# A recurrence, a mixture of experts and a feed-forward layer on one core: router steps, scatters and DMAs in another order

## The chip, the cores and the metric

The kernel runs on one core of a Trainium2 chip. The metric is the time of one execution in device microseconds (us); lower is better. In the text PE is TensorE, DVE is VectorE, ACT is ScalarE, POOL is GpSimd and SP is SyncE. SP computes nothing here: it issues most of the DMAs and reads register values.

## The reference

Three layers follow one another. Everything is float32.

```
# 1. recurrence over 768 steps, for 4 batches x 8 heads, head_dim 48
cur        = outer(u * k[t], v[t])
y[t]       = r[t] @ (state + cur)
state      = w[t][:, None] * state + outer(k[t], v[t])
# 2. x = y as 3072 tokens x 384; 8 experts, one per token
e          = argmax(x @ w_gate);  gate = softmax(x @ w_gate)[e]
x2[token]  = gate * sigmoid((x @ w_output_gate)[e]) * (relu(x @ w1[e]) @ w2[e])      # w1: 384x1024
# 3. dense layer, 384 -> 2048 -> 384
out        = relu(x2 @ w_in) ** 2 @ w_out
```

## The kernel before

**Stage 1, the recurrence (0 to about 180 us).** It is done in chunks of 128 steps. A unit is one pair of heads of one batch, so there are 16 units, and units 4b to 4b+3 are batch b. The loop over t runs from -1 to 16 and is a software pipeline: in one turn PE does the score products of unit t, the output of unit t-1, and the transposes of unit t+1. The order of the work on all five engines is the order of the calls in the text (a manual schedule), so an engine that waits holds everything behind it on that engine. The calls of one turn that matter here: `scores` (PE products into PSUM, ACT copies them to `A`, POOL masks them by an affine select, L734 to L737), `states` and `state_scan` (PE L744, DVE L749 into `St`), `suffix` and `prefix` (four DVE scans, L687 and L693), `k_turn` and `r_turn` (PE transposes L667, then DVE products `kT` L702 and `rA` L707), `gate_sum` and `gate_values` (DVE sum L717 of products that POOL made at L712 and L713, then POOL L720), `within` and `across` (PE L765 and L775, then ACT copies `xT` L777). The PSUM buffers of the transposes and the scores are one ring of four.

**The router.** When a batch is done, a generator (`route_steps`) computes its experts and ranks in 13 steps; two tables, `PLAN` for batches 0 and 1 and `LAST` for batch 2, say at which (turn, place) a step is taken; the places of a turn are "back", "scan", "turned", "gate" and "end". Steps 3 and 4 stand at (5, "scan") and hold small DVE operations and two ACT exponentials, `ez` (L188) and `sg` (L202). The last six steps each issue one scatter (POOL, L245) of 128 token rows into `x_rows` in DRAM, each row with 384 values, the gate factor and the token number. Batch 3 is routed after the loop.

**Stage 2, the experts (about 180 to 400 us).** Up to 320 tokens of expert 0 from batches 0 to 2 are block A; they are gathered (POOL, L400) after batch 2's scatters and worked on while batch 3 is routed. After batch 3's six scatters the experts are sorted by count. Block 0 is a rest of up to 128 tokens of expert 0, in rows (`up_rows`, `turn`, `down_rows`); blocks 1 to 7 are the other experts. A block's rows are gathered from `x_rows`, scaled (block 1's on DVE, L411), transposed on PE (`prep_x`, L430), and go through eight steps f of `up` (PE, 9 products of 128x128 weights, L344 to L346), a relu (ACT L333, DVE L334) and `down`. Each matrix is split into a high and a low float32r part (ACT cast L337, DVE or POOL difference L339). A block's words come in two halves of 1.5 MB (`load(0)`, `load(1)`: `w1r` L324 and `w2r` L325, two DMAs of 768 KB on SP); the first half serves f = 0 to 3.

**The order of DMAs on SP around the end of routing.** SP issues block 1's `load(0)`, then all engines pass a branch over rare cases (L941 to L942); at its end SP waits until all its own DMAs have landed. Then SP reads nine register values (L559, L562), stores block 0's token numbers (`put_ids`: 128 numbers of 4 bytes to `x2_ids`, L480), issues block 1's `load(1)`, the first load of a conversion (`convert_load`, `cq`, L1075), block A's results in three parts (`put_A`, L1238), with block 1's token numbers (384 and 96 of them, L480 and L484) ahead of the second part. The row gathers of blocks 0 and 1 are issued by POOL.

**Stage 3, the dense layer (about 400 to 846 us).** It goes over the 3072 tokens in 6 groups of 512, twice over halves of the 2048 columns, with PE in use throughout.

Of the kernel before, what the change touches and what calls it, by code (L numbers as in the profile page):

```python
# [9 lines left out]
F32 = mybir.dt.float32  # L10
# [11 lines left out]
def rwkv_moe_kernel(  # L22
# [15 lines left out]
    nc = tc.nc  # L38
# [522 lines left out]
    def expert_of(k):  # L561
        return nc.values_load(bei[0:1, k:k + 1], engines=(ET.SP,), min_val=0, max_val=E - 1)  # L562
# [13 lines left out]
    with ExitStack() as actx:  # L576
# [208 lines left out]
        def at(i, st, *a):  # L785
            if 0 <= i < NU:
                getattr(units[i], st)(*a)
# [1 line left out]
        PLAN = ((4, "gate"), (5, "back"), (5, "scan"), (5, "scan"), (6, "back"), (6, "scan"), (7, "scan"),  # L789
                (7, "turned"), (7, "gate"), (8, "back"), (8, "turned"), (9, "back"), (9, "turned"))  # L790
        LAST = ((4, "gate"), (5, "back"), (5, "scan"), (5, "scan"), (5, "turned"), (5, "gate"), (6, "scan"),
                (6, "scan"), (6, "turned"), (6, "gate"), (6, "end"), (7, "back"), (7, "scan"))

        def step(t, place):
            for b in range(B - 1):
# [42 lines left out]
        for t in range(-1, NU + 1):  # L838
            z = first_z if t == -1 else zw
            load("w", w, t + 3)  # L840
            if t >= 0:
                load("v", v, t + 1)
                load("k", k, t + 2)
                load("r", r, t + 2)
            first_block_step(t, "loads")
            at(t, "scores", 0)
            at(t, "k_back")
            at(t + 2, "w_check")
            step(t, "back")
            first_block_step(t, "back")  # L850
            if t + 1 < NU - 1:
                at(t + 1, "gate_products")
            at(t + 1, "suffix", 1, z)
            at(t + 1, "prefix", 1, z)
            at(t - 1, "within")
            at(t, "states")
            at(t, "state_scan")
            step(t, "scan")
            at(t, "scores", 1)
            at(t + 1, "spread")  # L860
            at(t - 1, "across")
            at(t + 1, "k_turn")
            at(t + 1, "r_turn")
            step(t, "turned")
            first_block_step(t, "turned")
            at(t + 2, "w_turn")
            at(t, "bonus_in")
            if t + 1 == NU - 1:
                at(t + 1, "gate_products")
            at(t + 1, "gate_sum")  # L870
            at(t + 1, "gate_values")
            at(t + 2, "suffix", 0)
            at(t + 2, "prefix", 0)
            step(t, "gate")
            first_block_step(t, "gate")
            if t < NU:
                at(t - 1, "back")
            step(t, "end")
# [27 lines left out]
    with tc.manual_schedule(engines={ET.PE, ET.DVE, ET.Activation, ET.SP, ET.Pool}):  # L906
        put_ids_A()
        blkA.prep_w(FA, nc.vector)
        route_step()
        route_step()  # L910
        blkA.up(0)
        route_step()
        route_step()
        route_step()
        blkA.up(1)
        nc.vector.tensor_scalar(flag[:, 0:1], pf[:1, :1], 0.0, None, op0=ALU.is_le)
        blkA.down(0)
        more = None
        while more is None:
            nc.gpsimd.memset(warm, 0.0)  # L920
            more = route_step()
        tc.mark_branch_hint_location("rare", "LikelyTaken", [ET.PE, ET.DVE, ET.SP])
        finish = finish_routing()
        next(finish)
        blkA.prep_w1(FA + 1, nc.vector)
        blkA.prep_w2(FA + 1, part="hi")
        for f in range(2, FA):
            blkA.up(f)
            if f == 2:
                next(finish)  # L930
                next(finish)
                blk1 = block_of(P, 1, expert_of(1))
                blk1.load(0)
            blkA.down(f - 1)
        for _ in finish:
            pass
        blkA.down(FA - 1)
# [261 lines left out]
    with tc.manual_schedule(engines={ET.PE, ET.DVE, ET.Activation, ET.SP, ET.Pool}):  # L1199
        block_rows()  # L1200
        blocks = [block_of(P, 0, 0), blk1]
        blk0 = blocks[0]
# [4 lines left out]
        for f in range(FA, KF):  # L1207
            blkA.up(f)
            if f + 2 < KF:
                blkA.prep_w(f + 2, nc.vector)  # L1210
            if f > FA:
                blkA.down(f - 1)
            if f == FA:
                blkA.prep_w2(FA + 1, nc.vector, part="lo")
            if f == FA + 1:
                for k in range(1, E):
                    if k == 1:
                        blk1.words_of(expert_of(k))
                    else:
                        blocks.append(block_of(P, k, expert_of(k)))  # L1220
                    blocks[k].banks((k + 1) % 2)
                blk0.put_ids(lambda: column(off, 0))
                blocks[1].load(1)
                convert_load(0)
            if f == KF - 1:
                blk0.prep_x(0)
# [18 lines left out]
        blk0.turn(0)  # L1245
        for f in range(2):
            blocks[1].prep_w1(f)
        blocks[1].put_ids(lambda: column(off, 1))
        put_A(1)
        convert_load(1)  # L1250
        put_A(2)
        blocks[1].prep_x(0)
        blk0.down_rows(0)
# [7 lines left out]
        for n in range(KF, E * KF):  # L1261
# [12 lines left out]
                nxt.gather(range(2 * f, min(2 * f + 2, nxt.nt)))  # L1274
            if e == 1 and f == 2:
                blk0.put(column(off, 0))
            if f == 2 and prev:
                prev.put(column(off, e - 1))
                if e == E - 1:
                    load_x(0)  # L1280
# [105 lines left out]
```

## Time and profile before

| what | value |
|---|---|
| median of 3 runs | 845.77 us (844.73 to 846.93) |
| the profiled execution's own time | 848.16 us |
| its span (first to last instruction) | 846.3 us |
| PE busy, share of the span | 808.7 us, 96% |
| PE weight loads | 733.0 us, 87% |
| DVE / ACT / POOL busy | 533.8 / 374.6 / 351.9 us |
| mean granted TensorE clock | 0.984 |
| HBM traffic, mean | 120 GB/s |

The profile page divides the span into 40 slices; PE is busy for nine tenths or more in nearly all of them, and less so in the first slice and in two slices around 180 and 210 us. The clock of TensorE has two levels, 1.2 and 2.4 GHz; the profile gives it as a share, 0.50 or 1.00 (or a mean of the two over a stretch). Busy time of PE is modelled at its ends, so the waits that the timeline notes beside an instruction, as [us <-who ended it], say more than the busy share.

### The profile page before, as it was taken

What the parts mean: (1) busy time and instruction counts of PE and PEld (TensorE: products, weight loads), DVE (VectorE), ACT (ScalarE), POOL (GpSimd) and SP (SyncE); (2) the same over time, 40 slices, a digit from 0 to 9 for tenths busy, and PEclk for the clock granted to TensorE, in tenths of its full rate; (3) what the DMA queues carried; (4) which work ended last, traced back from release to release, by engine and by line L of the source; (5) the groups of instructions that cost most, each with busy time, mean ns of one, the idle gap of its engine ahead of it and who ended that gap; (6) DMA issues with size and microseconds to landing.
All of it is one profiled execution on the core that took longest, in us unless ns stands there. A gap on an engine that the chain in (4) does not pass through costs nothing.

```text
span 846.3 us, 15487 instructions
## 1 busy us (share of the span) xinstructions
PE 808.7 (96%) x5868; PEld 733.0 (87%) x5868; DVE 533.8 (63%) x961; ACT 374.6 (44%) x792; POOL 351.9 (42%) x433
## 2 busy tenths in 40 slices
PE   6999999988799999999999999999999999999995
PEld 5988888868688999999999998888899999999994
DVE  7889888875367678787733788888633434434342
ACT  4666565632344554555554434343433333333321
POOL 8566767534245355555554234333311212223121
PEclk9999999999899999999999999999999999999998
DMA  8675759315967477577762232323204123032010
GB/s 179 131 151 108 168 116 222 134 53 161 151 189 213 129 246 209 151 227 237 151 195 63 94 112 65 105 79 108 75 1 140 35 79 112 9 104 76 1 47 37
DMA packets 157362, 102.89 MB, mean 122 GB/s; under 512 B 112348, under 2 KB 140940, under 8 KB 157284
## 3 DMA queue, kind: packets, MB, share of 16 engines
q1 hardware_dynamic: 149044, 86.55, 38.9%
q0 software_dynamic: 4912, 14.65, 5.0%
q8 instruction: 47, 0.77, 0.4%
q10 hardware_dynamic: 3328, 0.66, 0.4%
q14 instruction: 31, 0.25, 0.1%
HBM read 79.34 MB, written 22.50 MB: 120 GB/s over the span
## 4 chain that ended last, share of the span: by engine, by line
PE 69%; issue 13%; DVE 8%; POOL 4%; DMA 4%; ACT 1%; POOLq 0%; DVEq 0%; SPq 0%; ACTq 0%
PE ph L345 9%; PE ph L344 9%; PE ph L346 9%; PE po L344 5%; PE px L344 5%; PE px L346 5%; PE po L346 5%; PE po L345 5%; PE px L345 5%; POOL out_dram L1177 2%; PE py L765 2%; PE pt L667 2%; PE pt L734 2%; DMA xg<-x_rows,gi 2%; DMA x_rows<-xr,dsi 2%
## 5 line engine op out<-in xcount | busy, mean ns | idle before, releaser
L1152 DVE SCALAR_TENSOR_TENSOR gg<-ph,rl 128x512 f32<-128x512 f32 x96 | 66.2, 689 | 121.7 <-ACT rl L1150 121.7
L1150 ACT ACTIVATE rl<-ph 128x512 f32<-128x512 f32 x96 | 57.5, 599 | 146.5 <-PE ph L346 146.3
L339 DVE TENSOR_TENSOR gl<-gg,gh 128x512 fp32r<-128x512 f32 x96 | 66.8, 696 | 65.9 <-ACT gh L337 41.9
L337 ACT CAST gh<-gg 128x512 fp32r<-128x512 f32 x96 | 59.6, 621 | 103.5 <-DVE gg L1152 103.5
L339 POOL TENSOR_TENSOR w1l<-w1r,w1h 128x384 fp32r<-128x384 f32 x56 | 59.4, 1067 | 70.2 <-ACT w1h L337 69.7
L333 ACT ACTIVATE hh<-ph 128x320 fp32r<-128x320 f32 (+7 forms) x64 | 32.5, 508 | 112.9 <-PE ph L346 104.1
L1098 POOL TENSOR_TENSOR caf<-caf,cbf 128x384 f32<-128x384 f32 x32 | 32.6, 1018 | 114.0 <-DVE cbf L1097 114.0
L339 DVE TENSOR_TENSOR w2l<-w2r,w2h 128x384 fp32r<-128x384 f32 x64 | 64.9, 1016 | 20.0 <-ACT w2h L337 19.5
L334 DVE SCALAR_TENSOR_TENSOR hl<-ph,hh 128x320 fp32r<-128x320 f32 (+7 forms) x64 | 36.8, 576 | 36.9 <-ACT hh L333 36.6
L1177 POOL DMA_INDIRECT out_dram<-ob,tokc x24 | 23.4, 974 | 67.2 <-DVE ob L1175 65.0
L344 PE MATMUL po<-hh,w2h 128*128 128x320 f32 (+4 forms) x120 | 42.3, 353 | 0.0
L345 PE MATMUL po<-hl,w2h 128*128 128x320 f32 (+4 forms) x120 | 41.3, 345 | 0.0
L346 PE MATMUL po<-hh,w2l 128*128 128x320 f32 (+4 forms) x120 | 41.2, 344 | 0.0
L339 POOL TENSOR_TENSOR x22l<-x2r,x22h 128x512 fp32r<-128x512 f32 x12 | 15.5, 1293 | 51.5 <-ACT x22h L337 51.5
L737 POOL TENSOR_SCALAR_AFFINE_SELECT A<-A 128x768 f32<-128x768 f32 x32 | 27.9, 872 | 18.9 <-ACT A L736 18.8
L400 POOL DMA_INDIRECT xg<-x_rows,gi x28 | 28.9, 1033 | 15.6 <-DMA x_rows<-xr,dsi 9.3
L339 POOL TENSOR_TENSOR x21l<-x2r,x21h 128x512 fp32r<-128x512 f32 x12 | 15.5, 1294 | 45.5 <-ACT x21h L337 45.5
L734 PE MATMUL pt<-rA,kT 64*128 64x128 f32 x300 | 32.2, 307 | 2.1 <-DVE rA L707 2.1
L337 ACT CAST w2h<-w2r 128x384 fp32r<-128x384 f32 x64 | 33.0, 516 | 0.0
L245 POOL DMA_INDIRECT x_rows<-xr,dsi x24 | 24.4, 1019 | 20.2 <-DVE vals L238 14.1
L337 ACT CAST w1h<-w1r 128x384 fp32r<-128x384 f32 x64 | 32.7, 512 | 0.0
L339 POOL TENSOR_TENSOR x20l<-x2r,x20h 128x512 fp32r<-128x512 f32 x12 | 15.5, 1292 | 35.9 <-ACT x20h L337 35.9
(859 smaller groups left out, 2665.1 us busy)
## 6 DMA issues: line engine op xcount, KB each, us to landing
w1r<-in_moe_w_dram SPq DMA_DIRECT2D x16, 768.0 KB, 7.2
w2r<-in_moe_w_dram SPq DMA_DIRECT2D x16, 768.0 KB, 8.6
x2r<-x_cols SPq DMA_DIRECT2D x12, 768.0 KB, 4.9
cq<-in_moe_w_in_dram SPq DMA_DIRECT2D x16, 384.0 KB, 4.3
cq<-in_moe_w_out_dram SPq DMA_DIRECT2D x16, 384.0 KB, 5.9
vN<-in_v_dram SPq DMA_DIRECT2D x32, 144.0 KB, 3.9
part<-ob SPq DMA_DIRECT2D x24, 192.0 KB, 1.9
ob<-part SPq DMA_DIRECT2D x24, 192.0 KB, 2.5
```

Source lines behind the costliest of these rows:

```text
L333: nc.scalar.activation(hi, src, AF.Relu)
L334: nc.vector.scalar_tensor_tensor(lo, src, 0.0, hi.bitcast(F32), op0=ALU.max, op1=ALU.subtract)
L337: nc.scalar.copy(hi, src)
L339: lo_eng.tensor_tensor(lo, src, hi.bitcast(F32), op=ALU.subtract)
L344: nc.tensor.matmul(out_, a_of(ah), b_of(bh), start=start, stop=False)
L345: nc.tensor.matmul(out_, a_of(ah), b_of(bl), start=False, stop=False)
L346: nc.tensor.matmul(out_, a_of(al), b_of(bh), start=False, stop=stop)
L734: nc.tensor.matmul(pa[j][:, ci], self.kT[pp, hf * HC + ci], self.rA[pp, hf * HC + ci], start=True, stop=True)
L1098: nc.gpsimd.tensor_tensor(af, af, bf, op=ALU.add)
L1150: nc.scalar.activation(rl, ph, AF.Relu)
L1152: nc.vector.scalar_tensor_tensor(gg, ph, 0.0, rl, op0=ALU.max, op1=ALU.mult)
L1177: ins = nc.gpsimd.indirect_dma_start(out=out[:, :], out_offset=IndirectOffsetOnAxis(ap=tokc[:, n:n + 1], axis=0), in_=ob, in_offset=None)
```

## The change

Six things are done in another place; nothing is computed otherwise.

1. In a turn of the loop, the router steps of the place "scan" come after `scores(t, 1)`, `spread(t+1)` and `across(t-1)`, no longer before them.
2. Unit 0's `gate_sum` and `gate_values` come in turn 0 after unit 1's four scans, no longer in turn -1 ahead of them.
3. In `LAST` the last scatters of batch 2 come earlier: two at (6, "turned"), two at (6, "gate"), one at (7, "scan"), none at (6, "end") or (7, "back").
4. Ahead of block 1's `load(0)` SP issues a DMA of 4 bytes from `x_rows` into `spare`, a tile that nothing else of this path uses. As a reader of `x_rows` it waits for scatters of batch 3, and `load(0)` is queued behind it.
5. Block 0's and block 1's `put_ids` move from there to block 1's steps f = 2 and f = 3.
6. `convert_load(1)` comes ahead of the second part of block A's results.

```diff
         LAST = ((4, "gate"), (5, "back"), (5, "scan"), (5, "scan"), (5, "turned"), (5, "gate"), (6, "scan"),
-                (6, "scan"), (6, "turned"), (6, "gate"), (6, "end"), (7, "back"), (7, "scan"))
+                (6, "scan"), (6, "turned"), (6, "turned"), (6, "gate"), (6, "gate"), (7, "scan"))
...
             at(t + 1, "suffix", 1, z)
             at(t + 1, "prefix", 1, z)
+            if t == 0:
+                at(t, "gate_sum")
+                at(t, "gate_values")
             at(t - 1, "within")
             at(t, "states")
             at(t, "state_scan")
-            step(t, "scan")
             at(t, "scores", 1)
             at(t + 1, "spread")
             at(t - 1, "across")
+            step(t, "scan")
...
-            at(t + 1, "gate_sum")
-            at(t + 1, "gate_values")
+            if t >= 0:
+                at(t + 1, "gate_sum")
+                at(t + 1, "gate_values")
...
                 blk1 = block_of(P, 1, expert_of(1))
+                nc.sync.dma_start(spare[:, 0:1].bitcast(F32), x_rows[0:1, 0:1])
                 blk1.load(0)
...
-                blk0.put_ids(lambda: column(off, 0))
                 blocks[1].load(1)
                 convert_load(0)
...
-        blocks[1].put_ids(lambda: column(off, 1))
+        convert_load(1)
         put_A(1)
-        convert_load(1)
+        at1 = [column(off, 1)]
         put_A(2)
...
             if e == 1 and f == 2:
                 blk0.put(column(off, 0))
+                blk0.put_ids(lambda: column(off, 0))
+            if e == 1 and f == 3:
+                cur.put_ids(lambda: at1.pop() if at1 else column(off, 1))
```

DVE at the start of the loop, end of turn -1 and turn 0 (`g` is the gate sum, `suf` and `ff` are the scans of unit 1, `St` is unit 0's state scan):

```order
 L707 TENSOR_TENSOR rA<-pa,ff 128x6x64
+L687 SCALAR_TENSOR_TENSOR suf<-zw,s_142 128x388
+L692 RECIPROCAL f_141<-suf 128x3
+L693 SCALAR_TENSOR_TENSOR ff<-zw,f_141 128x387
+L687 SCALAR_TENSOR_TENSOR suf<-zw,s_142 128x388
+L692 RECIPROCAL f_141<-suf 128x3
+L693 SCALAR_TENSOR_TENSOR ff<-zw,f_141 128x387
 L717 TENSOR_REDUCE g<-g_256 128x12
```

The gate sum stood ahead of these six and now stands behind them, just ahead of the state scan.

ACT in the turn of batch 0's router steps 3 and 4, turn 5 (batches 1 and 2 alike, turns 9 and 13):

```order
 L178 COPY lg<-pt 128x2x3x16
+L736 COPY A_1213<-pt 128x3x128
+L736 COPY A_1213<-pa 128x3x128
+L697 COPY P_147<-suf 128x48x5
+L777 COPY xT<-py 128x384 x2
 L188 ACTIVATE ez<-z 128x48
 L202 ACTIVATE sg<-zs 128x6
-L736 COPY A_1234<-pt 128x3x128
-L736 COPY A_1234<-pa 128x3x128
-L697 COPY P_147<-suf 128x48x5
-L777 COPY xT<-py 128x384 x2
```

The two exponentials wait for DVE's router operations; they stood ahead of the copies of the scores and now stand behind them and behind the `xT` copies. On DVE the order of this turn is the same as before.

SP before, at the end of the register values after the rare branch:

```order
L559 TENSOR_LOAD off
L559 ISA x2
L480 REGISTER_ALU
L480 DMA x_ids<-xg_4903 128x1x1
L324 ISA
L324 DMA w1r<-in_moe_w_dram 128x3x512
L325 ISA
L325 DMA w2r<-in_moe_w_dram 128x4x384
L1075 DMA cq<-in_moe_w_in_dram 128x3x256
L1238 DMA x_cols<-yT 128x3x128
```

SP with the change, ahead of the rare branch (`spare`) and then in block 1's steps f = 2 and 3, after block 0's results (`yT_5294`):

```order
L946 TENSOR_LOAD flag
L946 ISA x2
L937 DMA spare<-x_rows 1x1
L324 ISA
L324 DMA w1r<-in_moe_w_dram 128x3x512
L325 ISA
L325 DMA w2r<-in_moe_w_dram 128x4x384
L947 COMPARE_AND_BRANCH
```

```order
L489 DMA x_cols<-yT_5294 128x3x128
L559 TENSOR_LOAD off
L559 ISA x2
L480 REGISTER_ALU
L480 DMA x_ids<-xg_4904 128x1x1
L480 REGISTER_ALU
L480 DMA x_ids<-xid 128x3x1
L559 TENSOR_LOAD off
L559 ISA x2
L484 ISA
L484 DMA x_ids<-xid 96x1
```

The small read stands ahead of the first half of block 1's words, and the three stores of token numbers are gone from the place between the register values and the second half.

## Rows read from the trace of the kernel before

**Rows 1.** Windows: PE, PEld, DVE, ACT, POOL busy us; PEclk, DMA share, GB/s.

```profile
200.00:250.00 50.00, 42.97 (x222) 38.10 (x220) 23.04 (x43) 20.57 (x49) 17.81 (x18) 0.92 0.72 154
```

**Rows 2.** Timeline of PE: start, us, line, operation [idle before <-releaser].

```profile
209.30 0.33 PE L430 MATMUL px<-ident,xg 128*128 128x128 f32 x1 [1.05 <-DMA xg<-x_rows,gi]
221.99 0.43 PE L430 MATMUL po<-ident,xg 96*128 96x96 f32 x1 [5.87 <-DVE xg L411]
222.12 0.67 PE L344 MATMUL px<-w2h,hh 128*128 128x384 f32 x1
225.79 0.60 PE L503 MATMUL px<-ident,hh 128*128 128x128 f32 x4
227.12 0.44 PE L344 MATMUL px<-w2h,hh 128*128 128x384 f32 x1
229.69 0.38 PE L344 MATMUL ph<-x0h,w1h 128*128 128x480 f32 x1
```

**Rows 3.** Windows of 2 us in that stretch.

```profile
216.00:218.00 2.00, 0.12 (x2) 0.00 (x0) 0.00 (x0) 1.29 (x3) 1.04 (x2) 1.00 0.88 52
222.00:224.00 2.00, 2.00 (x7) 1.89 (x8) 1.32 (x4) 0.56 (x1) 0.00 (x0) 0.50 1.07 389
```

**Rows 4.** Chain that ended last, 192 to 222 us: start us, us, what.

```profile
211.29 10.20 DMA xg<-x_rows,gi
```

**Rows 5.** Timeline of SP, its DMA issues, 188 to 262 us.

```profile
194.62 0.40 SPq L325 DMA_DIRECT2D w2r<-in_moe_w_dram  x1
210.77 0.57 SPq L480 DMA_DIRECT2D x_ids<-xg  x1
```

**Rows 6.** Timeline of POOL, last scatter and first gather after it.

```profile
195.97 0.97 POOL L245 DMA_INDIRECT x_rows<-xr,dsi  x1 [0.22 <-issue]
206.21 0.98 POOL L400 DMA_INDIRECT xg<-x_rows,gi  x1 [9.27 <-DMA x_rows<-xr,dsi]
```

**Rows 7.** Landing: tile x_rows (150 to 262 us), tile w2r (185 to 262).

```profile
DMA to landing us min/median/max: 2.6/3.9/10.2
DMA to landing us min/median/max: 9.3/9.3/9.4
```

**Rows 8.** DMA queues, 196 to 200 us: packets, MB, share.

```profile
q1 hardware_dynamic: 752, 1.32, 86.9%
q0 software_dynamic: 66, 0.21, 12.8%
```

**Rows 9.** SP, end of the rare branch: count, ns, first and last start.

```profile
L942 SPq EVENT_SEMAPHORE  x9: 17/17/17, 196.9 to 204.2; - x9
```

**Rows 10.** Timeline of ACT, block 1: words 4, rows of block 2.

```profile
234.58 0.51 ACT L337 CAST w1h<-w1r 128x384 fp32r<-128x384 f32 x1
246.33 2.13 ACT L413 ACTIVATE xg<-xg 128x384 f32<-128x384 f32 x4
```

**Rows 11.** Timeline of PE in the three units with router steps.

```profile
67.08 0.27 PE L667 MATMUL pt<-ident,rN 64*128 64x64 f32 x1 [0.93 <-ACT A L736]
107.42 0.97 PE L667 MATMUL pt<-ident,rN 64*128 64x64 f32 x12 [1.95 <-ACT A L736]
149.47 0.97 PE L667 MATMUL pt<-ident,rN 64*128 64x64 f32 x12 [1.94 <-ACT A L736]
```

**Rows 12.** Timeline of DVE after the third of them.

```profile
150.41 1.02 DVE L707 TENSOR_TENSOR rA<-pt,ff 128x384 f32<-128x384 f32 x2 [0.51 <-PE pt L667]
158.09 0.76 DVE L749 TENSOR_TENSOR_SCAN St<-pt,P 128x288 f32<-128x288 f32 x1 [0.60 <-PE pt L744]
```

**Rows 13.** Timeline of DVE, then of PE, at the start of the kernel.

```profile
13.13 0.75 DVE L717 TENSOR_REDUCE g<-g 128x12 f32<-128x576 f32 x1 [2.03 <-POOL g L713]
18.74 0.37 PE L667 MATMUL pt<-ident,kN 64*128 64x64 f32 x1 [1.25 <-DVE St L749]
```

**Rows 14.** Timeline of PE, then of POOL, in the last unit.

```profile
173.24 0.88 PE L765 MATMUL py<-A,vN 128*64 128x128 f32 x12 [2.37 <-POOL bia L920]
174.81 0.99 POOL L400 DMA_INDIRECT xg<-x_rows,gA  x1 [1.61 <-DVE w2l L339]
```

## The prediction

> **What bounds the kernel now.** I read the page first (PE is busy almost throughout), then the windows by stage, which show where it is not: between 200 and 250 us PE is busy for 42.97 of 50 us at a mean granted clock of 0.92 [rows 1], and after 250 us no slice has a gap. Then the timeline of PE, for each wait and what ended it. The reader is to see that four small groups of waits in the first 230 us are all that an order can win; after them PE runs without a pause to the end, so a microsecond won before 230 us is a microsecond of the whole.
>
> The largest wait is at 216.1 to 222.0 us: PE waits 5.87 us for the last of block 1's gathered rows [rows 2]. The chain says why: that gather left POOL at 211.29 and took 10.20 us [rows 4], against 2.6 us for the quickest DMA on that table [rows 7]. It was issued 0.52 us after SP had stored block 0's token numbers (210.77, [rows 5]). In the middle of that time the DMA engines are busy for 0.88 of their time and move only 52 GB/s, where they move 389 GB/s six microseconds later [rows 3]. What fills them with next to nothing is, I read, the store of 128 numbers of 4 bytes. After this wait the granted clock stands at 0.50 (1.2 GHz) [rows 3], and the 12 products that follow take 3.67 us (222.12 to 225.79) where the next 12 of the same kind take 2.57 us (227.12 to 229.69) [rows 2].
>
> Ahead of that, POOL issues the last scatter at 195.97 and waits until 206.21 for them to land [rows 6], while SP's first half of block 1's words, issued up to 194.62 [rows 5], flows beside them.
>
> **The change part by part.**
>
> *Unit 0's gate sum.* DVE waits 2.03 us for POOL's products ahead of four scans; PE waits 1.25 us for the state scan behind them [rows 13]. With the sum behind the scans, POOL's products are ready before DVE comes to them, so the 2.03 us go. Late next is PE itself, which stood still for only 1.25 us. I take 1.2 us; the ends are 0 (another input is late) and 2.0.
>
> *Router steps 3 and 4 later on ACT.* In three turns PE waits for ACT's copies of the scores, 0.93, 1.95 and 1.94 us [rows 11], since ACT sits before `ez` and `sg`, which wait for DVE. Behind the copies they hold nobody: their results are read by router steps that come at least a place later. DVE's order is unchanged, so DVE caps the gain where it is nearly full: after the third turn its idle time is 0.51 + 0.60 = 1.11 us [rows 12]. Hence 0.9 + 1.9 + 1.1 = 3.9 us. The ends: 1.5 us (0.51 us per turn, if DVE decides everywhere) and 4.8 us (the three waits in full).
>
> *Batch 2's scatters.* PE waits 2.37 us for POOL's last mask, which stands behind scatters; block A's gather leaves at 174.81 [rows 14]. With the scatters earlier the mask comes some 2 us earlier, but block A's first transposes and, behind them, batch 3's logits still need the gathered rows, and one scatter stays between mask and gather. PE's wait moves to those rows. I take 0; the ends are 2.4 us and a loss of 1.0 us, about the clock's price after the other wait (3.67 - 2.57 us).
>
> *The small read ahead of block 1's words.* It adds one DMA of 4 bytes and a wait on SP for scatters. The last one leaves POOL's queue at 195.97 + 0.97 and should land 2.6 to 3.9 us after its start [rows 6, 7], so near 199.5 where POOL saw them landed at about 206. The words then leave near 200.3 and 201 where they left at 194.62, and POOL's gathers of blocks 0 and 1 leave between about 200.5 and 206. So the words no longer run beside the scatters, but beside the gathers. Between 196 and 200 us the words' queue moved 752 packets and the scatters' 66 [rows 8]: the gathers will creep until the words are in, 9.4 us after their issue [rows 7], near 210.4. Block 0's rows may come as late as before, where PE waits 1.05 us [rows 2]: I take 0, between a gain of 1.05 and a loss of 2 us (landing 1 us after the words). The Trainium skill, "DMA: Bandwidth & Descriptors", section "Queues, rings and completion order", says that each DMA engine takes turns between the queues that have work, packet by packet. By that rule the gathers would get their turn beside the words and the 1.05 us would go; the trace's 66 against 752 packets speak against equal turns.
>
> Behind the waiting SP stand the words, the rare branch and all that follows it. At the end of that branch SP waits for its own DMAs, before until 204.2 [rows 9], now until about 210.4. From there it needed 6.6 us of register reads and one wait to reach its next DMA (210.77); so the second half of the words leaves near 217 and lands by 226.4. ACT casts the first of them at 234.58 [rows 10], 7.0 us earlier by the sum below, 227.6. That is free by 1.2 us; if it lands 3 us later than that, it costs about 2 us.
>
> *Token numbers later.* The two blocks' stores leave the time of the gathers, and nothing else clogs the engines there: the last of block 1's rows can be in by about 214, before PE wants it at 216.1. So the 5.87 us go, and with them the 1.1 us at the low clock: 7.0 us. The ends are 0 (the gathers creep until PE waits as long) and 7.0. The three stores are not saved: they follow in block 1's steps 2 and 3, behind block 0's results and block 2's first words on the same queue, where no wait of PE shows now. The moved conversion load is needed 20 us later and costs nothing.
>
> *Sum.* 1.2 + 3.9 + 0 + 0 + 7.0 = 12.1 us. The profiled execution's own time is 848.16 us, 2.4 above the median of the runs; against it this is 836.1, and against the median of 845.77 it is **833.7 us**.
>
> **The rivals.**
>
> 1. *Equal turns on the DMA engines.* The gathers share evenly with the words, as the rule above has it, and block 0's wait goes too: 833.7 - 1.05 = 832.6 us. Against it stands the share of packets [rows 8].
>
> 2. *The wait only moves.* The gathers creep behind the words and SP's late second half adds to it, so PE waits as long for rows or words as it did for the last gather; only the recurrence gains: 845.8 - 1.2 - 3.9 = 840.7 us. For it: the scatters that ran beside the words landed late [rows 6]. Against it: 5 us lie between the words' landing and PE's need.
>
> 3. *DVE takes over in the recurrence.* The waits of PE for ACT become waits for DVE and only the expert stage gains: 845.8 - 7.0 = 838.8 us. For it: 1.11 us of idle time after the third turn. Against it: PE's waits at the other two are longer than DVE's work behind them asks.
>
> 4. *The stores hold up block 2's rows, and the kernel gets slower.* Block 2's rows are gathered in block 1's steps 0 and 1 and scaled on ACT at 246.33 [rows 10], or 239.3 when shifted. The stores would come near 229.5. If a store holds a gather as the one at 210.77 held the last one until 221.5, for 10.7 us, and the three of them do so in turn, the rows land at 229.5 + 32.1 = 261.6: a wait of 22.3 us and 1.1 for the clock, less 12.1, is 857 us. It decides from rows later than about 253 on; two stores in turn (250.9) would make the time that of before. Against it: block 2's last gather leaves about when the first store does, ahead of most of their writes.
>
> 5. *It doesn't do what it says.* The read waits for only some of the scatters, or the late landing had another cause, and no wait goes: 845.8 us.
>
> **How the numbers follow.** Forecast 0.64, rival 1 0.08, rival 2 0.14, rival 3 0.06, rival 4 0.04, rival 5 0.04. About 0.3% (2.5 us) is what a measurement of this kernel tells from no change. The first four cases are faster: 0.92; rival 5 is the same, 0.04; rival 4 slower, 0.04. All upper ends together (2.0 + 4.8 + 2.4 + 1.05 + 7.0 = 17.2) would give 828.6, which asks for everything at once; I take 829. Upwards the range reaches to rival 2, 841. It leaves out rivals 4 and 5 and the tails of the rest, under 2 in 10.
>
> **What would show each step.** In the changed profile: DVE's gate sum of unit 0 behind the scans with no wait of 2 us; ACT's copies of the scores ahead of `ez` in turns 5, 9 and 13 and no wait of PE of 0.9 to 2 us there; the wait of PE for POOL's mask in the last unit gone, and one for block A's rows in its place; the words of block 1 issued after the scatters have landed, POOL's first gather of block 0 some 6 us nearer to the last scatter; block 1's last rows landing without a stretch of full DMA engines at 50 GB/s, and no wait of 5.87 us nor a clock of 0.50 behind it; that stretch in block 1 instead, without a wait of PE. The prediction is wrong if block 0's or block 1's rows still arrive after PE asks for them by more than 2 us, if ACT waits for the second half of the words, or if the turns of the recurrence are as long as before.

## The result, and the profile after

The changed kernel takes 837.37 us (median of 4 runs, 836.17 to 837.66), the kernel before on the same chip 846.35 us (844.73 to 848.15): a ratio of 0.9891, 95% interval 0.9867 to 0.9914, 9.0 us faster. The forecast was 833.7 us with a range of 829 to 841. The profiled execution of the changed kernel has a span of 835.6 us, 10.7 less than before. Single times of one kernel spread by 0.6 to 6.4 us, those of the kernel before by more (841.7 to 853.8 over all its runs). So a verdict is taken from medians, and a microsecond is read from traces, each of which shows one execution only.

The windows of the changed kernel (columns as in [rows 1]), the stage of [rows 1] first, then the end of the recurrence:

```profile
200.00:250.00 50.00, 49.47 (x259) 42.89 (x258) 29.90 (x53) 24.05 (x56) 20.17 (x21) 1.00 0.64 177
...
170.00:174.00 4.00, 0.49 (x4) 0.14 (x1) 1.10 (x3) 0.37 (x1) 2.66 (x3) 1.00 0.39 105
174.00:178.00 4.00, 2.85 (x14) 1.60 (x16) 2.42 (x9) 1.18 (x3) 0.00 (x0) 0.50 0.11 19
178.00:182.00 4.00, 4.00 (x23) 3.25 (x19) 1.93 (x9) 1.47 (x5) 0.00 (x0) 0.50 0.01 0
182.00:186.00 4.00, 4.00 (x18) 3.82 (x18) 2.54 (x14) 0.45 (x2) 0.00 (x0) 0.50 0.00 0
186.00:190.00 4.00, 4.00 (x24) 4.00 (x24) 2.62 (x13) 1.67 (x4) 3.19 (x6) 0.80 0.28 99
```

Between 200 and 250 us PE is now busy for 49.47 us at full clock (42.97 at 0.92 before, [rows 1]). But there is a new hole: from 170 to 174 us PE works for 0.49 of 4 us, and behind it the granted clock stands at 0.50 (1.2 GHz) until about 187.6 us.

The timeline of PE in the changed kernel: the first `within`, the last `across` but one, the last router products, block A's rows, the branch, block 0's rows, block 1's last rows, block 1's first product.

```profile
22.46 1.53 PE L765 MATMUL py<-A,vN 128*64 128x128 f32 x24
...
162.49 1.41 PE L775 MATMUL py<-rA,St 64*64 64x128 f32 x20
...
168.26 1.93 PE L169 MATMUL pt<-xT,wcat 128*32 128x256 f32 x24
173.53 0.30 PE L430 MATMUL pt<-ident,xg 128*128 128x128 f32 x1 [3.34 <-DVE xg L411]
174.74 0.47 PE L430 MATMUL pt<-ident,xg 128*128 128x128 f32 x1 [0.91 <-DVE xg L411]
175.50 1.28 PE L430 MATMUL pt<-ident,xg 64*128 64x64 f32 x4 [0.28 <-DVE xg L411]
...
195.95 0.38 PE L344 MATMUL ph<-x0h,w1h 128*128 128x320 f32 x1 [1.29 <-PEq L947]
205.31 0.27 PE L430 MATMUL px<-ident,xg 128*128 128x128 f32 x1
211.57 0.57 PE L430 MATMUL po<-ident,xg 128*128 128x128 f32 x4
212.46 0.44 PE L344 MATMUL px<-w2h,hh 128*128 128x384 f32 x1 [0.31 <-ACT hh L337]
...
218.96 0.38 PE L344 MATMUL ph<-x0h,w1h 128*128 128x480 f32 x1
```

In the kernel before the same points lie like this on PE (up to the branch; block 0's rows and block 1's first product are in [rows 2]):

```profile
24.67 1.53 PE L765 MATMUL py<-A,vN 128*64 128x128 f32 x24
...
167.01 1.40 PE L775 MATMUL py<-rA,St 64*64 64x128 f32 x20
...
176.38 2.50 PE L169 MATMUL pt<-xT,wcat 128*32 128x256 f32 x24
...
179.84 0.33 PE L430 MATMUL pt<-ident,xg 128*128 128x128 f32 x1 [0.70 <-DVE xg L411]
180.63 0.84 PE L430 MATMUL pt<-ident,xg 64*128 64x64 f32 x4 [0.46 <-DVE xg L411]
...
197.20 0.38 PE L344 MATMUL ph<-x0h,w1h 128*128 128x320 f32 x1 [1.97 <-PEq L942]
```

So PE is 2.2 us early at 22 us, 4.5 us early at the last `across` but one, 8.1 us early at the router's last products, only 1.25 us early at the branch, and 10.7 us early at block 1's first product (229.69 in [rows 2]). From there to the end both traces take 616.6 us. Neither the 1.05 us wait for block 0's rows nor the 5.87 us wait for block 1's is left [rows 2]. For block A's rows PE now waits 3.34 + 0.91 + 0.28 = 4.5 us, where it waited 0.70 + 0.46 = 1.2 us before.

What PE waits for between 20 and 165 us in the changed kernel (us in total, times, longest): the three waits of [rows 11] for ACT's scores, 4.8 us in all, are gone. Waits for DVE have come in their place, 5.1 us in the list below, where the kernel before has 1.0 us of them in the same window. The longest, 1.95 us at 144.30 us, stands in the turn of the third wait of [rows 11].

```profile
PE pt L209 <- DVE kT L702: 1.9, 1, 1.9
PE pt L734 <- DVE rA L707: 1.7, 5, 0.3
PE pt L667 <- DVE kT L702: 1.0, 3, 0.6
PE pt L209 <- ACT A L736: 0.5, 2, 0.3
PE pa L667 <- DVE kT L702: 0.5, 1, 0.5
```

The timelines of POOL (block A's first gather, the last scatter, block 0's first gather) and of SP (the read, block 1's first words, its second half, the token numbers) in the changed kernel, for [rows 5, 6, 14]:

```profile
169.77 1.00 POOL L400 DMA_INDIRECT xg<-x_rows,gA  x1 [3.73 <-issue]
192.84 0.97 POOL L245 DMA_INDIRECT x_rows<-xr,dsi  x1 [0.22 <-issue]
198.82 1.07 POOL L400 DMA_INDIRECT xg<-x_rows,gi  x1 [5.00 <-DVE hl L334]
```

```profile
195.49 0.30 SPq L937 DMA_DIRECT2D spare<-x_rows  x1
196.06 0.44 SPq L324 DMA_DIRECT2D w1r<-in_moe_w_dram  x1
...
210.71 0.39 SPq L324 DMA_DIRECT2D w1r<-in_moe_w_dram  x1
...
226.28 0.58 SPq L480 DMA_DIRECT2D x_ids<-xg  x1
237.38 0.41 SPq L480 DMA_DIRECT2D x_ids<-xid  x1
```

The gather follows the last scatter by 5.98 us (198.82 - 192.84), where it was 10.24 us [rows 6]. Block A's gather is only 5.0 us earlier than in [rows 14], although PE comes to it 8.1 us earlier: POOL stands 3.73 us between the last scatter (164.88) and the gather, and the gathered rows are what DVE, and behind it PE, wait for. I take the 3.73 us for the landing of that scatter, but the trace has no landing time for it, and those just ahead of it landed in 2.6 to 2.7 us; so it is not shown that the landing is all of it.

### The profile page after: what moved, and what is told of

Read it like the earlier page. It is cut to its first block, busy times and chain, and to the rows that moved or that the text cites. A ratio compares the mean times of both kernels' runs of the same rounds, so it can differ in the third digit from the quotient of the medians.

```text
span 835.6 us, 15492 instructions
## 1 busy us (share of the span) xinstructions
PE 805.9 (96%) x5868; PEld 731.1 (87%) x5868; DVE 534.2 (64%) x961; ACT 374.3 (45%) x792; POOL 352.3 (42%) x433
## 4 chain that ended last, share of the span: by engine, by line
PE 59%; issue 12%; POOL 4%; DVE 0%; POOLq 0%; ACT 0%; DVEq 0%; ACTq 0%
PE ph L345 10%; PE ph L344 10%; PE ph L346 10%; PE po L344 5%; PE po L346 5%; PE po L345 5%; PE px L346 5%; PE px L344 5%; PE px L345 5%; POOL out_dram L1182 2%; PE px L430 1%; PE po L430 0%; POOL x22l L339 0%; POOL x21l L339 0%; POOL x20l L339 0%
```

## The experiments

The theory at this point: two chains of work race to block 0's rows. One is PE's own. The other goes through block A's rows, batch 3's logits, its scatters and block 0's gathers. What the recurrence won is partly lost in the hole at 170 us and at the low clock behind it, and it is lost on the second chain too, since batch 3's logits stand behind block A's rows on PE. Rivals are the prediction's own sum, each term worth what it said, and that the hole costs nothing. All experiments ran beside the kernel before; the ratio is that of the times to it. They ran in three sets on three chips, where the kernel before took 847.36, 847.40 and 847.45 us, so times of different sets are compared as they are. The intervals of the ratios reach 2 to 3 us to either side, so a difference of 2 us between two of these kernels is not settled by the times alone.

### The changed kernel again

> The changed kernel once more, on the chip of the next three, as their base: 837.4 us (its first four runs) plus or minus 0.7.

Measured: 838.24 us, ratio 0.9895 (0.9871 to 0.9919). The second trace is worth more than the time. PE behind the branch and at block 0's rows in it:

```profile
192.97 0.38 PE L344 MATMUL ph<-x0h,w1h 128*128 128x320 f32 x1 [1.36 <-PEq L947]
204.72 0.33 PE L430 MATMUL px<-ident,xg 128*128 128x128 f32 x1 [2.22 <-DMA xg<-x_rows,gi]
```

Here the clock was back at 1.00 from 182 us on, PE passed the branch 3.0 us sooner than in the first trace, and then waited 2.22 us for block 0's rows, with a granted clock of 0.69 behind that wait (206 to 210 us). The span is 836.6 against 835.6 us. The two chains thus end within about 2 us of each other, and a gain on one alone is soon covered by the other.

### Parts taken out of the change

Without the read:

```diff
-                nc.sync.dma_start(spare[:, 0:1].bitcast(F32), x_rows[0:1, 0:1])
```

> The changed kernel without the read of one number of x_rows ahead of block 1's first words. Theory: the read is a term of its own. Without it the 2 MB of words start at once after the branch's first instructions, lie beside batch 3's scatters, block 0's first gather goes to about 206 instead of 198.8, PE again waits about 1 us for block 0's rows and about 0.7 us more behind the branch, and the granted clock falls again at 198 to 202 (about 1.5 us): 3 us in all, 840 to 841. Rival (the prediction's own sum): the read is worth nothing, since block 1's rows are held up by the token numbers alone: 837.4 plus or minus 0.7, and PE meets block 1's rows without a wait. A third way: without the read the words still lie in the queues when block 1's gathers go, and block 1's rows wait some us with no token number in the queue: 842 or more.

Measured: 840.62 us, 0.9931 (0.9908 to 0.9953), 2.4 us slower than with the read (times from 837.66 to 841.90, with it from 835.77 to 839.72). Its trace is of the fastest of its runs and shows no loss. The first gather goes at 200.40 instead of 198.82 us though the last scatter left at 192.64, but PE is the late chain there: it meets block 0's rows without a wait at 205.51 us and comes to block 1's first product at 219.16 us. The theory's size holds, its 206 for the gather does not. That the 2.4 us of the other runs are waits for block 0's rows is not shown.

With the token numbers in the old places (part 6, the conversion load, goes back with them):

```diff
+                blk0.put_ids(lambda: column(off, 0))
                 blocks[1].load(1)
...
+        blocks[1].put_ids(lambda: column(off, 1))
+        put_A(1)
         convert_load(1)
-        put_A(1)
-        at1 = [column(off, 1)]
         put_A(2)
...
                 blk0.put(column(off, 0))
-                blk0.put_ids(lambda: column(off, 0))
-            if e == 1 and f == 3:
-                cur.put_ids(lambda: at1.pop() if at1 else column(off, 1))
```

> The changed kernel with the token numbers of blocks 0 and 1 (and the first conversion load) back at their old places on SP, the read kept. The prediction gave the later places 7.0 us: then this is 844.4. Theory now: with the read SP comes to the first token numbers only at about 210.5, when all rows of blocks 0 and 1 have landed, so no row waits; but the second half of block 1's words is queued behind them on SP and lands about 5 to 10 us later, where ACT wants it at about 224: a wait of 0 to 7 us on PE at block 1's up(2) or up(3), 837.5 to 843, and none at block 1's rows. Rival: the two edits overlap wholly, the words are early enough: 837.4 plus or minus 0.7.

Measured: 843.16 us, 0.9954 (0.9933 to 0.9974): 5.0 us slower, not 7.0. SP, then DVE, then PE in this trace:

```profile
209.32 0.57 SPq L480 DMA_DIRECT2D x_ids<-xg  x1
210.16 0.41 SPq L324 DMA_DIRECT2D w1r<-in_moe_w_dram  x1
```

```profile
226.51 0.36 DVE L1090 TENSOR_SCALAR ca<-cq 128x384 int32<-128x384 int32 x1 [4.55 <-DMA x_ids<-xid]
```

```profile
229.15 0.49 PE L345 MATMUL po<-hl,w2h 128*128 128x480 f32 x1 [3.30 <-DVE hl L334]
```

Block 1's rows come without a wait, as the theory says. The loss is behind them, 3.30 us on PE and a clock of 0.53 after it (230 to 232 us), but the late transfer that DVE stands for is not the words. The view names a store of token numbers; the instruction itself reads `cq`, the first conversion load, one place behind the words on SP's queue, so I take it for that load. From 212 to 218 us, behind the first store, the engines move 49 to 63 GB/s, where the changed kernel has 389 from 214 to 216 us:

```profile
214.00:216.00 2.00, 1.89 (x14) 1.45 (x13) 1.26 (x3) 1.88 (x5) 0.00 (x0) 1.00 0.64 63
```

With the router's steps in the old places:

```diff
-                (6, "scan"), (6, "turned"), (6, "turned"), (6, "gate"), (6, "gate"), (7, "scan"))
+                (6, "scan"), (6, "turned"), (6, "gate"), (6, "end"), (7, "back"), (7, "scan"))
...
+            step(t, "scan")
             at(t, "scores", 1)
             at(t + 1, "spread")
             at(t - 1, "across")
-            step(t, "scan")
```

> The changed kernel with the router's steps in the recurrence back at their old places (the old list for batch 2, and the 'scan' steps again ahead of the second score half). The prediction gave this part 3.9 us (0.9 + 1.9 + 1.1, and 0 for batch 2's scatters): then this is 841.3. Theory now: at the end of the recurrence PE was 8.7 us early, of that 2.2 from the start, but block A's rows came only 5 us early, PE stood 4.5 us for them and the granted clock stayed at 0.50 for 13 us; at the branch PE is only 1.25 us early, 0.7 of it the branch itself. So all of the router's gain and more was given back: 835.5 to 838.0, with the waits for ACT back in the recurrence, and the clock at 0.50 for no more than about 4 us in 170 to 190.

Measured: 840.18 us, 0.9918 (0.9891 to 0.9945): by the medians the part is worth 1.9 us, between the theory (nothing) and the prediction (3.9 us). With times from 837.28 to 842.73 us neither is excluded. The wait for the mask is back (2.34 us at 170.47), the hole ahead of block A's rows is 1.28 us, and the clock still falls, to 0.73 and 0.85 between 178 and 186 us.

With unit 0's gate sum in its old place (the two `if` lines around `gate_sum` and `gate_values` undone):

> The changed kernel with unit 0's gate sum back in its old place, so that DVE waits for POOL's products before unit 0's last scans. The prediction gave this place 1.2 us (839.4 where the changed kernel has 838.2); the profile of the changed kernel says that PE was 2.2 us early from 22 us on, with nothing that takes it back before the end of the recurrence: 840.4. Rival: the recurrence, or the scatters behind it, take it back: 838.2 plus or minus 0.7.

Measured: 837.82 us, 0.9879 (0.9844 to 0.9914): the median shows no loss, as the rival has it, though its interval of 3 us to either side doesn't exclude the 1.2 us. The trace leans the other way: PE's last router products come at 169.42 instead of 168.26 or 166.91 us, the last scatter at 194.87 instead of 192.84 or 192.36, and block 1's first product at 220.34 instead of 218.96 or 219.98 us. So some 0.4 to 1.4 us reach the end in this one execution.

### The hole filled

```diff
         route_step()
+        scratch = ps_t.tile([128, 512], F32, name="pt")
+        for n in range(36):
+            g, pr = n % 3, n // 3 % HP
+            nc.tensor.matmul(scratch[32 * g:32 * g + 32, :S // 3], wcat[:, pr], xTs[B - 1][:, pr, g * (S // 3):(g + 1) * (S // 3)],
+                             start=True, stop=True)
         blkA.prep_x(0)
```

> The changed kernel with 36 more router products into a scratch tile that nothing reads, on PE between its last router products and block A's first rows, where it stands 3.3 to 4.2 us: about 2.9 us of work at full clock, nothing left out. It tests the idle time's price through the granted clock alone (the waits for the rows stay). Theory: the clock stays at 1.00 or comes back sooner, the logits and batch 3's first scatter come 1 to 2 us sooner, and as block 0's rows, which come out of these scatters, end the race against PE at 205, the time falls by what the scatters gain and no more: 836 to 837.5 where the changed kernel has 838.2. Rival A: the clock is the whole loss, PE gets back 4 us of the 13 us at 0.50: 833.5 to 835. Rival B: the clock falls all the same, or block 0's rows come no sooner: 838.2 plus or minus 0.7.

Measured: 834.87 us, 0.9846 (0.9807 to 0.9885), 3.4 us faster than the changed kernel for doing more work. It falls into rival A's range. Its windows:

```profile
170.00:174.00 4.00, 4.00 (x53) 2.05 (x47) 1.75 (x5) 0.00 (x0) 1.88 (x2) 1.00 0.43 124
174.00:178.00 4.00, 3.34 (x28) 2.46 (x28) 2.93 (x12) 2.24 (x7) 0.00 (x0) 1.00 0.06 4
178.00:182.00 4.00, 4.00 (x28) 3.58 (x28) 2.98 (x17) 1.56 (x5) 0.00 (x0) 1.00 0.01 0
```

The clock stays at 1.00. The last scatter leaves at 189.76 us instead of 192.84 or 192.36, 2.6 to 3.1 us sooner, and PE still waits 1.86 us for block 0's rows: so the gain is about what the scatters gained, as the theory has it, but I had put that at half its size.

The same with the router's steps in the old places (12 products, for a hole of 1.28 us):

> The changed kernel with the router's steps at their old places (840.2 us), and 12 router products into a scratch tile in the 1.3 us for which PE stands ahead of block A's rows there. It tells whether the moved router steps are worth what the prediction gave them (3.9 us) once the clock is kept in both: the changed kernel with such products has 834.9. Theory: the clock falls less here (0.73 and 0.85 from 178 to 186), so the products give 0.5 to 1.5 us, 838.7 to 839.7, and the router's steps are worth 3.9 to 4.8 with the clock kept. Rival: the products give 3 us here too (837), and the steps are worth 2 us, clock or no clock.

Measured: 837.54 us, 0.9882 (0.9846 to 0.9919). The products give 2.6 us here too, though the clock had fallen less: nearer to the rival. With both holes filled, the moved router steps are worth 837.54 - 834.87 = 2.7 us. The clock is not kept throughout here: PE still waits 2.39 us for the mask, and behind it the granted clock is 0.59 from 170 to 174 us; after that it is 1.00.

### Batch 3's router ahead of block A's rows

```diff
         route_step()
+        route_step()
+        units[-1].back()
+        route_step()
+        route_step()
+        blkA.scale(nc.vector)
         blkA.prep_x(0)
         blkA.prep_x(1)
-        route_step()
-        units[-1].back()
         blkA.prep_x(2)
+        route_step()
...
+        route_step()
+        route_step()
         blkA.prep_w(FA, nc.vector)
-        route_step()
-        route_step()
         blkA.up(0)
-        route_step()
-        route_step()
-        route_step()
         blkA.up(1)
```

(The scaling of block A's rows in the last turn's "back" place is taken out there.)

> The changed kernel with batch 3's router ahead of block A's rows: the logits' transposes, the turn back of the last unit, the max, one-hot, gate and count steps come before block A's rows are scaled and turned, the counts' products right behind these, and the destination steps ahead of up(0). Nothing is left out. Theory: batch 3's scatters decide (block 0's rows come out of them). The logits are there from 170.6, where they now wait for block A's rows until 177.3: the first scatter goes at 179 to 182 instead of 185.7 to 186.4, block 0's rows are there before PE, and PE itself has 1.3 us less to do behind the idle time: 832.5 to 836 where the changed kernel has 838.2. Rival: it is PE and its clock that decide up to the branch, and the scatters were early enough: 837.0 to 838.2. Other side: scaling block A's rows behind the router's steps on DVE makes block A late: 839 or more.

Measured: 833.23 us, 0.9825 (0.9786 to 0.9863), as the theory had it. POOL's first scatter of batch 3 and its first gather of block 0, then PE:

```profile
180.54 1.05 POOL L245 DMA_INDIRECT x_rows<-xr,dsi  x1 [7.91 <-DVE w1l L339]
...
194.59 1.07 POOL L400 DMA_INDIRECT xg<-x_rows,gi  x1 [6.62 <-DVE hl L334]
```

```profile
172.89 0.30 PE L430 MATMUL pt<-ident,xg 128*128 128x128 f32 x1 [2.70 <-DVE xg L411]
...
201.09 0.27 PE L430 MATMUL px<-ident,xg 128*128 128x128 f32 x1
```

The scatters are 5.1 to 5.8 us earlier than in the changed kernel (185.65 and 186.38), block 0's rows are there when PE asks, and PE is now the bound, with 2.70 us of the hole left. Its five times lie within 0.6 us.

Both together, with 27 products in what is left of the hole:

> The kernel with batch 3's router ahead (833.2 us, ratio 0.9825), and 27 router products into a scratch tile that nothing reads in the 2.7 us for which PE still stands ahead of block A's rows. Theory: the clock, at 0.54 to 0.60 from 174 to 182 there, stays at 1.00: PE gets back 2.5 to 3 us, and block 0's rows have 2 us of slack: 830.5 to 832. Rival: block 0's rows end the race now, 833.0 plus or minus 0.4 with a wait of 2 us or more for them.

Measured: 830.73 us, 0.9811 (0.9774 to 0.9847), the fastest here; the clock is 1.00 from 170 us on, and block 0's rows come without a wait at 197.75 us.

### Parts added to the kernel before

The later token numbers alone, the read alone, and both:

> The kernel before with one part of the change alone, the token numbers of blocks 0 and 1 (and the first conversion load) at their later places. The prediction gave it 7.0 us (5.87 of waiting for block 1's last rows and 1.1 of the clock behind it): ratio 0.9917, 840. By what the changed kernel lost without it (838.2 to 843.2) it is 5.0: ratio 0.994, 842. Rival: the wait only moves, since the second half of the words then goes earlier, beside block 1's gathers: ratio 0.998 to 1.000.

Measured: 845.98 us, 0.997 (0.9943 to 0.9996): 1.4 us, a fifth of the 7.0 and nearest to the rival. The trace is of the slowest of its runs (848.64 us). In it SP comes to block 1's second half of the words at once, beside block 0's and block 1's gathers, and the wait moves to another transfer:

```profile
211.45 0.39 SPq L324 DMA_DIRECT2D w1r<-in_moe_w_dram  x1
```

```profile
213.47 0.93 POOL L400 DMA_INDIRECT xg<-x_rows,gi  x1 [0.31 <-issue]
```

```profile
220.62 0.33 PE L430 MATMUL po<-ident,xg 128*128 128x128 f32 x1 [2.22 <-DVE xg L411]
221.68 0.42 PE L430 MATMUL po<-ident,xg 96*128 96x96 f32 x1 [0.74 <-DVE xg L411]
```

With no store ahead of them, the words and rows flow:

```profile
214.00:216.00 2.00, 2.00 (x11) 1.59 (x10) 1.37 (x5) 0.89 (x3) 0.41 (x1) 1.00 1.04 393
```

Beside the 52 GB/s of [rows 3] and the 63 GB/s above, both with a store issued some 5 us before, this bears out what the prediction read there: it is the store that fills the engines with next to nothing.

> The kernel before with one part of the change alone, the read of one number of x_rows ahead of block 1's first words. Prediction's sum: 0 (846.4 to 847.4, ratio 1.000). Theory now: the read lets batch 3's scatters land ahead of the words, so block 0's gathers go about 5 us sooner and SP comes to the token numbers when most rows have landed; the wait of 5.87 us for block 1's last rows is gone with the token numbers still in their old place, but block 1's second half of the words comes late behind them, as in the changed kernel with the old places (3.3 us of waiting there): ratio 0.995 to 0.998. Rival: the token numbers hold the rows all the same, 1.000 plus or minus 0.001, with 4 us or more of waiting for block 1's rows.

Measured: 847.95 us, 1.000 (0.9975 to 1.0024). Every wait is as the theory said, and the sum is nil all the same: the wait for block 1's rows is gone, and 2.82 us have come behind the token numbers.

```profile
216.29 0.58 PE L430 MATMUL po<-ident,xg 128*128 128x128 f32 x4
...
235.01 0.48 PE L345 MATMUL po<-hl,w2h 128*128 128x480 f32 x1 [2.82 <-DVE hl L334]
```

> The kernel before with the two parts of the change at the branch and behind it (the read and the later token numbers), and none of those in the recurrence. The later numbers alone gave 0.997, without the read the wait only moved, from the token numbers to the words. Theory: the two parts need one another, and together they give 7 to 8 us: ratio 0.991, no wait for block 1's rows, and next to no wait for block 0's. Rival: they only add up, 0.997 and what the read alone gives in the run beside this.

Measured: 843.84 us, 0.9946 (0.9919 to 0.9973; single times in two heaps, 838.8 to 840.2 and 842.1 to 844.7). The middle lies between theory (0.991) and rival (0.997), and the interval does not decide. Block 1's rows come without a wait; 1.91 us for block 0's remain, with a clock of 0.58 behind.

### What all the traces say together

| kernel | last scatter | PE behind the branch | wait for block 0's rows | block 1's first product | from there to the end |
|---|---|---|---|---|---|
| before | 195.97 | 197.20 | 1.05 | 229.69 | 616.6 |
| before, numbers later | 198.07 | 199.20 | 1.44 | 230.17 | 616.6 |
| before, read | 196.14 | 196.78 | 2.12 | 223.66 | 621.2 |
| before, read and numbers | 198.27 | 198.82 | 1.91 | 225.53 | 616.7 |
| changed, first trace | 192.84 | 195.95 | 0 | 218.96 | 616.6 |
| changed, second trace | 192.36 | 192.97 | 2.22 | 219.98 | 616.6 |
| read left out | 192.64 | 196.15 | 0 | 219.16 | 616.6 |
| numbers in old places | 191.97 | 194.34 | 0 | 217.33 | 621.7 |
| router in old places | 194.29 | 194.84 | 2.11 | 221.73 | 616.7 |
| gate sum in old place | 194.87 | 197.23 | 0 | 220.34 | 616.7 |
| hole filled | 189.76 | 190.36 | 1.86 | 215.44 | 616.7 |
| router in old places, hole filled | 192.96 | 193.51 | 2.20 | 218.97 | 616.7 |
| router ahead | 187.00 | 191.73 | 0 | 214.74 | 616.7 |
| router ahead, hole filled | 185.03 | 188.39 | 0 | 211.42 | 616.7 |

The last column is the span less the column ahead of it. Everything the change does lies before block 1's first product, but for the token numbers in their old place behind a read: 4.6 to 5.1 us. The last scatter is the better mark than PE: from it to block 1's first product it takes 33.7 us before, 26.1 and 27.6 in the two traces of the changed kernel. So the read with the later numbers brought 6.1 to 7.6 us behind the last scatter (in the one trace without the read it is 26.5 us too). What the recurrence brought ahead of it differs from one execution to the next: the first four kernels of the table do the same work on PE, DVE, ACT and POOL up to the last scatter, and it leaves between 195.97 and 198.27 us; the two traces of the changed kernel and those without the read and with the numbers in old places share another one, and it leaves between 191.97 and 192.84 us. That is 3.1 to 6.3 us.

## Why the prediction was right, and where it was off

The direction and the range were right: 837.4 us lies between 829 and 841, 3.7 us above the forecast. That the sum came so near is in part luck, since no term came out in the time as it was put: by the medians three were put too high, and the read, put at nothing, made up for some of it. One sign of being wrong that the prediction named came true in one of two traces: block 0's rows arrived 2.22 us after PE asked for them, where it had set 2 us.

- *The later token numbers, 7.0 us.* They cost 5.0 us in the changed kernel, but alone only 1.4. The mechanism was half of it. The gathers left late, and whatever SP issued beside them held them up: the stores for the 5.87 us of [rows 2], or, without the stores, the second half of the words for 2.22 + 0.74 us. With the read alone the gathers are early and no wait for block 1's rows is left, but the stores then hold up the conversion load. Rival 2, "the wait only moves", is what happens in the kernel before without the read. The term belonged to both edits together, 6.1 to 7.6 us by the traces.
- *The small read, 0.* Worth 2.4 us in the changed kernel, by the medians, and nothing alone. The step that failed is that "the gathers will creep until the words are in", near 210.4 us. In the changed kernel the scatters had landed when the read went at 195.49, SP passed on at once, and the gathers were not held: between 198 and 206 us they had 32.8% of the engines' time and the words 56.5% (270 and 900 packets), where it had been 12.8 and 86.9% for the scatters beside the words [rows 8], and they landed in 3.3 to 6.3 us. The Trainium skill, "DMA: Bandwidth & Descriptors", section "Queues, rings and completion order", has the engines take turns between queues, packet by packet; this stretch comes nearer to that than [rows 8], without showing equal shares. Block 0's wait went in one trace and became 2.22 us in the other.
- *The second half of the words.* Forecast to leave near 217, it left at 210.71, since the first half was in long before 210; ACT never waits for it.
- *Unit 0's gate sum, 1.2 us.* PE won 2.2 us by it at 22 us, more than PE's 1.25 us of standing still, since products behind it took less time too (the six of L758 ahead of that point 0.82 us, before 1.49). The median gained nothing (837.82 against 838.24), and the trace 0.4 to 1.4 us: the size of the term is open.
- *The router's steps on ACT, 3.9 us.* The waits for ACT went, and DVE took part of them over, as the term allowed. At the last `across` but one, ahead of the wait for the mask, PE was 4.5 us early (162.49 against 167.01), and 5.9 us in the second trace (161.14), where start and router had been put at 5.1: the size was right at that point. In the time the steps are worth 1.9 us with batch 2's scatters, 2.7 with both holes filled.
- *Batch 2's scatters, taken at 0 (ends +2.4 and -1.0): the other step that failed.* It had the mechanism, the wait for the mask goes and one for block A's rows comes, but not the size. The mask's wait of 2.37 us went in full, and the waits for block A's rows grew from 1.2 to 4.5 us, since the last scatter and three gathers set those rows, however early PE is. So PE stands still for about 1 us more, and the rest is the clock: behind the hole it stayed at 0.50 for 8 to 14 us (before, behind the mask's wait, only from 174 to 177.6). Filling the hole gave 3.4 us back. The end of -1.0 us had been taken from the clock's price of 1.1 us in one short stretch, [rows 2]; here that price was two to three times as much. No run takes this part out alone, so what it is worth by itself stays open.
- *No rival 4.* The stores now stand between 226 and 246 us, and PE is busy throughout.

Summed by what taking each part away cost, 0 + 1.9 + 2.4 + 5.0 = 9.3 us; the change gave 9.1 beside x1's runs. That the two agree is partly chance, since read and numbers need one another.

## What to carry to other kernels

Before a wait is priced, ask how many transfers would each cause it alone; two such edits have one price together, and little apart. When a stage ends in a chain of landing, routing and gathering, follow that chain and not the busiest engine: in the first trace PE was 8 us early at its start, and the last scatter only 3, and what helped was to put the router's small steps ahead of the rows that were not there yet (833.2 us), then to keep PE busy in the hole that was left (830.7 us).

## What the runs showed of the hardware

- A store of 128 numbers of 4 bytes is dear out of all proportion: block 0's took 11.1 us to land, where 768 KB of words took 9.3 [rows 7], and what is queued behind such a store crawls (52 and 63 GB/s, against 393 and 389 without it). The landings that the view of the tile `x_ids` has, 220 to 262 us of the changed kernel, are of block 0's 128 numbers (the middle one) and of 384 numbers each of blocks 1 and 2:

```profile
DMA to landing us min/median/max: 7.7/11.1/12.5
```

  SP issued the second one 11.10 us after the first (226.28 and 237.38), as it did before (210.77 in [rows 5], and 222.04). That SP waits until the first has landed, as both go to the same table, is inferred from the equal times; the third store, which the kernel's text exempts from waiting for the second, left 1.2 us after it (238.59). In the changed kernel no wait of PE shows in that time.
- The hole of 4.5 us cost most through the clock. PE's work behind it ran at 1.2 GHz until 187.6 us in one execution and until about 181 in another of the same kernel, busy nearly all that time; filled with products that nobody needs, the hole cost 3.4 us less. Why one execution took 6 us longer to come back stays open. The Trainium skill, "TensorE: Matmul & The Clock Gate", section "HAM oscillation — how this bites in real kernels", says of a matmul loop over small tiles that a wait for a DMA between pieces of work lets the next one start at the low clock, and that doing more of the work ahead of such a wait, or a larger tile, cures it. The hole, with 0.50 behind it, agrees with the first; the cure that ran here is another one, the filled hole, and the clock was 1.00 behind it.
